# The check of the bounds' bits in a top-k attention kernel: once at the end on a kept copy, not once per batch

## The chip, the cores and the metric

The kernel runs on one core of one Trainium2 chip. The metric is device time in microseconds (us), the median of several runs. The engines are called as in the profile: PE is TensorE (PEld its weight loads), DVE is VectorE, ACT is ScalarE, POOL is GpSimd, SP is SyncE, which issues most DMAs.

## The reference

Eight batches of top-k attention with 8 heads, 576 tokens and a head width of 64, and behind it a mixture-of-depths layer:

```python
scores = scale * np.matmul(q, k.transpose(0, 1, 3, 2))
kth = np.partition(scores, -top_k, axis=-1)[..., -top_k:-top_k + 1]   # top_k = 32
scores = np.where(scores >= kth, scores, -1000000000.0)
...                                                                   # softmax, times v
x = attn_out.transpose(0, 2, 1, 3).reshape(B, S, H * D)               # 8 x 576 x 512
scores = np.einsum('bsd,d->bs', x, w_gate)
out = x.copy()
for b in range(B):
    top_idx = np.argpartition(-scores[b], capacity)[:capacity]        # capacity = 128
    xe = x[b, top_idx]
    ye = np.maximum(xe @ w1, 0.0) @ w2
    out[b, top_idx] = x[b, top_idx] + sigmoid(scores[b, top_idx])[:, None] * ye
```

## The kernel before

**Units.** The attention is cut into 144 units, 18 per batch; a unit is 128 score rows twice (two heads, `i` = 0 and 1), each of 576 scores. The main loop (line 1094) runs over steps `n`, one unit entering at each, and works as a pipeline: in step `n` PE turns the scores of unit n-4 (`weigh`) and multiplies those of unit n+1, ACT takes the exponent (`pT`, `last`), copies the scores out (`sc`), and compares unit n-1 with its bound (`sides`); POOL makes `y` from that and half of the mask `less`; DVE searches.

**The search.** DVE does not look for the 32nd largest score at once. `find_bound` takes a bound near it from parts of the row (maxima of `cand`, then `best`, then `bound`); ACT and POOL work out which scores lie under the bound and how many (`sides`, `seen`, `y`), and `find_kth` takes the 8 largest of `y` (`next8`), the last of which is the 32nd largest. This is exact only if a few things hold. They are gathered as the kernel goes, and checked at the end: `seen` (the counts), `sums` (softmax sums), `ranks`, `others`, and `least`, which is the change's place. If the check fails, the branch at line 1368 computes everything again in a plain way (`general`); with the inputs here it isn't taken.

**The bounds' check.** `keep_least` (line 1073) is called from `mask_of` in the step in which the last unit of a batch gets its mask, for seven batches within the loop, and once more at line 1255. It takes the batch's 36 bounds (18 units, two heads) and 36 32nd-largest values, which lie in `bounds[b]` and `next8s[b]`. DVE looks at the low 23 bits of each bound (`low`: 0 would mean a bound that is a power of two), and reduces bounds, values and `low` to one number each in `least[:, 0:3, b]`.

**The order.** All engines are wrapped in `InOrder`, so each executes its instructions in the order in which the code emits them. Work that is to stand later in an engine's queue is kept in lists of closures: `late` (run by `flush`, mostly ACT's), `vector_late` (`flush_vector`, inside `find_bound`), `pool_late`. In the loop `flush()` stands at line 1127, right behind `mask_of(n - 3)` and ahead of the `sc` copy. The mixture of a batch (`mixture`, line 599) is a generator that is stepped through the loops of the next batches: gate scores (`prod`, line 943, on DVE, which reads `x`, made by POOL), ranks (`junk`), places, rows fetched (`xe`), h and y matmuls.

**The end.** After the loop the last batch's mixture is done by `closing` (line 746), a generator too, with the end of the batch before it (`between`) in it. At its fourth `yield` (line 830, just after `flush()`) the code comes to line 1255: `keep_least` for the last batch, and the chain of reductions that multiplies all checks into `sure`. The following `next(closed)` (line 1295) puts the transposes of `xe` and the `xeT` copy in the queues; `count_unsure()` then puts a matmul of `sure` and `ones` into PE's queue; the next `next(closed)` emits h, y and the scatter of the last rows.

Of the kernel before, what the change touches and what calls it, by code (L numbers as in the profile page):

```python
# [11 lines left out]
ALU = mybir.AluOpType  # L12
FP32 = mybir.dt.float32
BF16 = mybir.dt.bfloat16
I32 = mybir.dt.int32
# [11 lines left out]
LEAST = 1.0e-16 * SMALLER  # L27
# [21 lines left out]
def kernel(  # L49
# [12 lines left out]
    P = nc.NUM_PARTITIONS  # L62
    B, H, S, D = q.shape
# [14 lines left out]
    const = ctx.enter_context(tc.tile_pool(name="const", bufs=1))  # L78
# [4 lines left out]
    stats = ctx.enter_context(tc.tile_pool(name="stats", bufs=6))  # L83
    ptpool = ctx.enter_context(tc.tile_pool(name="pt", bufs=2))
    xpool = ctx.enter_context(tc.tile_pool(name="x", bufs=2))
    modpool = ctx.enter_context(tc.tile_pool(name="mod", bufs=1))
# [43 lines left out]

    NS = B * 2 * (J * NHP + NHP // 2)
    seen = const.tile([P, NS], FP32, name="seen")
    least = const.tile([P, 3, B], FP32, name="least")
    sums = const.tile([P, B * NT, H], FP32, name="sums")
    nc.gpsimd.memset(sums, 1.0)

# [31 lines left out]
    def load_weights():  # L168
# [6 lines left out]
    pe, dve, act, pool, sp = (  # L175
        InOrder(tc, e)
        for e in (nc.tensor, nc.vector, nc.scalar, nc.gpsimd, nc.sync)
    )


    late, vector_late, pool_late = [], [], []
# [5 lines left out]
    def flush():  # L187
        while late:
            late.pop(0)()
# [148 lines left out]
    def groups(t):  # L338

        return NHP // 2 if t == J else NHP  # L340
# [638 lines left out]
    per_batch = sum(groups(t) for t in range(NT))  # L979
# [27 lines left out]
    for b in range(B - 1):  # L1007
        n = (b + 1) * per_batch + mix_at_of.get(b, mix_at)[6]
# [62 lines left out]
        find_kth(ys.pop(n), next8s[b][:, i, :, :])  # L1071

    def keep_least(b, bound, kth):
        low = stats.tile([P, per_batch, 2], I32, name="low", bufs=1)
        dve.tensor_scalar(
            out=low,
            in0=bound.bitcast(I32),
            scalar1=(1 << 23) - 1,
            scalar2=1,
            op0=ALU.bitwise_and,  # L1080
            op1=ALU.bitwise_xor,
        )
        for w, of in enumerate((bound, kth, low)):
            dve.tensor_reduce(
                out=least[:, w, b : b + 1], in_=of, axis=mybir.AxisListType.XY, op=ALU.min
            )

    def mask_of(n, on=None):
        b, i = divmod(n, per_batch)
        masks[n] = mask(scs[n], next8s[b][:, i, :, :], on)  # L1090
        if i == per_batch - 1 and b < B - 1:
            keep_least(b, bounds.pop(b)[:, :, :, 7], next8s.pop(b)[:, :, :, 7])

    for n in range(-1, N):
        b, i = divmod(n, per_batch)
# [32 lines left out]
        if is_unit(n + 1):  # L1128
            b, t, g = units[n + 1]
            ps = room_for_scores()  # L1130
            kT, qT = qkv[b][0:2]
            b, i = divmod(n, per_batch)
# [42 lines left out]
        if gating is not None:  # L1175
            b, t = gating
# [5 lines left out]
        b, i = divmod(n, per_batch)  # L1182
# [70 lines left out]


    keep_least(B - 1, bounds.pop(B - 1)[:, :, :, 7], next8s.pop(B - 1)[:, :, :, 7])
    sure = stats.tile([P, 1], FP32, name="sure")
    dve.memset(sure, 1.0)
    for what, op, than, limit in (
        (least[:, 0, :], ALU.min, ALU.is_gt, LEAST),
        (least[:, 1, :], ALU.min, ALU.is_gt, LEAST),  # L1260
        (least[:, 2, :], ALU.min, ALU.is_gt, 0.5),
        (seen, ALU.max, ALU.is_lt, float(MIDDLE)),
        (seen, ALU.min, ALU.is_gt, float(MIDDLE - 16)),
        (sums.rearrange("p t h -> p (t h)"), ALU.min, ALU.is_gt, FEWEST),
        (sums.rearrange("p t h -> p (t h)"), ALU.max, ALU.is_lt, MOST),
    ):
        far = stats.tile([P, 1], FP32, name="far")
        dve.tensor_reduce(out=far, in_=what, axis=mybir.AxisListType.X, op=op)
        dve.scalar_tensor_tensor(
            out=sure, in0=far, scalar=limit, in1=sure, op0=than, op1=ALU.mult  # L1270
        )
# [133 lines left out]
```

## Time and profile before

| | |
|---|---|
| median of 3 runs | 826.69 us (826.53 to 827.79) |
| the profiled execution | 828.44 us; its span 826.1 us |
| granted TensorE clock over the span | 0.99 of full |
| DVE busy | 787.2 us (95%) |
| POOL busy | 715.4 us (87%) |
| ACT busy | 730.7 us (88%) |
| PE busy | 777.0 us (94%), ends modelled |
| DMA | 50.38 MB, mean 61 GB/s |
| `low` | 8 instructions, 175 / 1060 / 1231 ns (least, median, most) |
| `least` from bounds, values, `low` | 8 each, median 207, 200, 172 ns |

A timeline line reads: start in us from the span's start, duration, engine, source line (L45 is the wrapper, so tiles tell more than lines), operation, output tile <- input tiles, shapes, count; in brackets the idle time of the engine before it and what ended it. A line of waits reads: who waited <- for whom: us in total, times, longest. An engine counts as busy from the start to the end of an instruction, also where the instruction stands still in between.

### The profile page before, as it was taken

What the parts mean: (1) busy time and instruction counts of PE and PEld (TensorE: products, weight loads), DVE (VectorE), ACT (ScalarE), POOL (GpSimd) and SP (SyncE); (2) the same over time, 40 slices, a digit from 0 to 9 for tenths busy, and PEclk for the clock granted to TensorE, in tenths of its full rate; (3) what the DMA queues carried; (4) which work ended last, traced back from release to release, by engine and by line L of the source; (5) the groups of instructions that cost most, each with busy time, mean ns of one, the idle gap of its engine ahead of it and who ended that gap; (6) DMA issues with size and microseconds to landing.
All of it is one profiled execution on the core that took longest, in us unless ns stands there. A gap on an engine that the chain in (4) does not pass through costs nothing. (4 is left out here: it accounts for less than half of the span.)

```text
span 826.1 us, 28252 instructions
## 1 busy us (share of the span) xinstructions
PE 777.0 (94%) x10143; PEld 596.5 (72%) x10143; DVE 787.2 (95%) x4651; ACT 730.7 (88%) x1557; POOL 715.4 (87%) x722
## 2 busy tenths in 40 slices
PE   6888888888999999999999999999999999999976
PEld 5566666666887778877787777877787777767744
DVE  7899999999999999999999999999999999999960
ACT  4799999999999999999999999999999999879831
POOL 3799999999899999999899999999999998899831
PEclk9699999999999999999999999999999999999999
DMA  7931111521141221521223221512215102101021
GB/s 170 283 86 40 28 66 28 105 53 27 60 92 36 53 40 59 112 47 34 79 47 86 53 40 60 104 23 54 40 59 112 28 15 66 23 12 18 2 71 30
DMA packets 122133, 50.38 MB, mean 61 GB/s; under 512 B 116417, under 2 KB 116417, under 8 KB 120961
## 3 DMA queue, kind: packets, MB, share of 16 engines
q1 hardware_dynamic: 118672, 43.91, 22.0%
q0 software_dynamic: 1728, 4.20, 2.8%
q8 instruction: 82, 1.34, 0.8%
q14 instruction: 67, 0.54, 0.3%
q10 hardware_dynamic: 1584, 0.39, 0.2%
HBM read 36.93 MB, written 11.55 MB: 59 GB/s over the span
## 5 line engine op out<-in xcount | busy, mean ns | idle before, releaser
L45 POOL TENSOR_TENSOR y<-sc,sides 128x576 f32<-128x576 f32 x288 | 365.1, 1289 | 57.0 <-ACT sides L45 54.3
L45 DVE MAX8 cand<-sc 128x8 f32<-128x82 f32 (+1 forms) x2016 | 314.0, 228 | 2.7 <-ACT sc L45 2.7
L45 POOL TENSOR_SCALAR less<-sc,next 128x576 bf16<-128x576 f32 x135 | 232.5, 1722 | 12.9 <-DVE next L45 10.0
L45 PE MATMUL ptr<-out_of_reach,less 128*128 128x128 bf16 x1136 | 205.3, 220 | 19.5 <-POOL less L45 19.4
L45 ACT ACTIVATE sides<-sc,bound 128x576 bf16<-128x576 f32 x288 | 223.0, 787 | 0.0
L45 PE MATMUL ptr<-ident,sc 128*128 128x128 f32 x1136 | 217.0, 282 | 0.0
L45 DVE MAX8 next<-y 128x8 f32<-128x584 f32 x288 | 204.4, 751 | 1.7 <-POOL y L45 1.6
L45 PEld LDWEIGHTS av<-v,pT 128*64 128x64 f32 x4544 | 144.1, 137 | 66.9 <-ACT last L45 63.2
L45 PE MATMUL ps<-kT,qT 64*128 64x288 f32 (+1 forms) x1280 | 182.0, 431 | 5.2 <-ACT qT L45 5.2
L45 PEld LDWEIGHTS ptr<-ident,sc 128*128 128x128 f32 x1136 | 161.3, 142 | 29.1 <-issue 17.4
L45 ACT ACTIVATE pT<-ptr 128x1024 f32<-128x1024 f32 x142 | 145.3, 1023 | 33.2 <-PE ptr L45 32.2
L45 PE MATMUL av<-v,pT 128*64 128x65 f32 x4544 | 163.7, 224 | 9.3 <-ACT last L45 8.5
L45 ACT COPY sc<-ps 128x1152 f32<-128x1152 f32 (+1 forms) x144 | 162.2, 1126 | 3.5 <-PE ps L45 3.5
L45 PEld LDWEIGHTS <-less 128*128 128x128 bf16 x1296 | 136.1, 106 | 39.2 <-POOL less L45 25.2
L45 PEld LDWEIGHTS ps<-kT,qT 64*128 64x128 f32 (+1 forms) x1280 | 100.2, 178 | 41.5 <-issue 21.2
L45 ACT ACTIVATE less<-sc,next 128x576 bf16<-128x576 f32 x143 | 111.2, 777 | 12.7 <-DVE next L45 10.8
L45 DVE MATCH_REPLACE8 cand<-best,cand 128x21 f32<-128x21 f32 (+1 forms) x576 | 99.0, 180 | 0.0
L45 DVE MAX8 best<-cand 128x8 f32<-128x21 f32 (+1 forms) x576 | 90.5, 190 | 0.0
L45 PE MATMUL h_ps<-xeT,w 128*128 128x128 f32 x464 | 65.8, 286 | 0.0
L45 PEld LDWEIGHTS h_ps<-xeT,w 128*128 128x128 f32 x464 | 55.8, 191 | 9.2 <-issue 5.8
L45 PE MATMUL y_ps<-w,hT 128*128 128x512 f32 x112 | 60.6, 636 | 0.0
L45 ACT ACTIVATION_READ_ACCUMULATOR sides<-sc,bound 128x1 f32 x288 | 59.9, 208 | 0.0
(133 smaller groups left out, 866.4 us busy)
## 6 DMA issues: line engine op xcount, KB each, us to landing
v<-in_v_dram SPq DMA_DIRECT2D x64, 128.0 KB, 4.2
out_dram<-x SPq DMA_DIRECT2D x8, 1024.0 KB, 3.9
rows<-in_k_dram SPq DMA_DIRECT2D x56, 128.0 KB, 2.9
rows<-in_q_dram SPq DMA_DIRECT2D x56, 128.0 KB, 3.1
w<-in_moe_w_dram SPq DMA_DIRECT2D x2, 2048.0 KB
gate_row<-row_dram SPq DMA_DIRECT2D x7, 288.0 KB, 4.4
w<-in_k_dram SPq DMA_DIRECT2D x8, 128.0 KB, 3.2
last<-in_k_dram SPq DMA_DIRECT2D x8, 128.0 KB, 4.0
```

The costliest lines, as they stand in the source:

```text
L45: return lambda *a, **kw: self._tc.keep_in_program_order(fn(*a, **kw))
```

## The change

Within the loop DVE keeps one reduction per batch, that of the 32nd-largest values. ACT copies the batch's 36 bounds to `bounded`, a tile of 288 numbers that is kept to the end; the copy goes through `late`, and so stands behind ACT's half of the mask and ahead of the `sc` copy. At the end, after the last copy, DVE makes `low` for all 288 bounds in one operation, and the check reduces `bounded` and `low` (288 wide each) and `least` (8 wide) in place of three rows of `least`. `low` shares its space with `junk` and `prod` (tag `scratch`).

```diff
     seen = const.tile([P, NS], FP32, name="seen")
-    least = const.tile([P, 3, B], FP32, name="least")
+    least = const.tile([P, B], FP32, name="least")
+    bounded = const.tile([P, NS], FP32, name="bounded")
...
     def keep_least(b, bound, kth):
-        low = stats.tile([P, per_batch, 2], I32, name="low", bufs=1)
-        dve.tensor_scalar(
-            out=low,
-            in0=bound.bitcast(I32),
-            scalar1=(1 << 23) - 1,
-            scalar2=1,
-            op0=ALU.bitwise_and,
-            op1=ALU.bitwise_xor,
-        )
-        for w, of in enumerate((bound, kth, low)):
-            dve.tensor_reduce(
-                out=least[:, w, b : b + 1], in_=of, axis=mybir.AxisListType.XY, op=ALU.min
-            )
+        at = 2 * per_batch * b
+        late.append(
+            lambda: act.copy(
+                out=bounded[:, at : at + 2 * per_batch].rearrange("p (n i) -> p n i", i=2),
+                in_=bound,
+            )
+        )
+        dve.tensor_reduce(
+            out=least[:, b : b + 1], in_=kth, axis=mybir.AxisListType.XY, op=ALU.min
+        )
...
     keep_least(B - 1, bounds.pop(B - 1)[:, :, :, 7], next8s.pop(B - 1)[:, :, :, 7])
+    flush()
+    low = modpool.tile([P, S], I32, name="low", tag="scratch")[:, 0:NS]
+    dve.tensor_scalar(
+        out=low,
+        in0=bounded.bitcast(I32),
+        scalar1=(1 << 23) - 1,
+        scalar2=1,
+        op0=ALU.bitwise_and,
+        op1=ALU.bitwise_xor,
+    )
     sure = stats.tile([P, 1], FP32, name="sure")
     dve.memset(sure, 1.0)
     for what, op, than, limit in (
-        (least[:, 0, :], ALU.min, ALU.is_gt, LEAST),
-        (least[:, 1, :], ALU.min, ALU.is_gt, LEAST),
-        (least[:, 2, :], ALU.min, ALU.is_gt, 0.5),
+        (bounded, ALU.min, ALU.is_gt, LEAST),
+        (least, ALU.min, ALU.is_gt, LEAST),
+        (low, ALU.min, ALU.is_gt, 0.5),
         (seen, ALU.max, ALU.is_lt, float(MIDDLE)),
```

PE's, POOL's and SP's instructions and their order stay as they were. DVE has three instructions less per batch in the loop; ACT has one more.

## The prediction

> **What bounds the kernel now.** I read the page's first part, then busy time by stretch and waits by engine, one batch, the places where the removed instructions stood, and the end. The page:
>
> ```profile
> PE 777.0 (94%) x10143; PEld 596.5 (72%) x10143; DVE 787.2 (95%) x4651; ACT 730.7 (88%) x1557; POOL 715.4 (87%) x722
> ```
>
> This invites one reading: VectorE (DVE) is the bound, so take work off it. The stretch of one batch in the middle (stretch, length, then busy time of PE, PEld, DVE, ACT, POOL) and all waits of ACT over 0.15 us in it say more:
>
> ```profile
> 392.32:488.42 96.10, 94.93 (x1267) 73.59 (x1266) 95.99 (x577) 91.50 (x197) 88.52 (x88) 1.00 0.27 60
> ```
>
> ```profile
> ACT pT L45 <- PE ptr L45: 4.0, 11, 0.6
> ```
>
> DVE has no gap in 96.1 us. But ACT is busy or waiting for TensorE (91.5 + 4.0) for 95.5 of them, and TensorE's weight loads wait for ACT (8.1 us for `last`). ACT and PE hand work to each other and set 96.1 us as much as DVE does. How can DVE be just as full? The timeline at the end of a batch shows it (start, duration):
>
> ```profile
> 306.11 1.06 DVE L45 TENSOR_SCALAR low<-bound 128x36 int32<-128x36 int32 x1
> 307.10 0.20 DVE L45 TENSOR_REDUCE least<-bound 128x1 f32<-128x36 f32 x1
> 307.23 0.20 DVE L45 TENSOR_REDUCE least<-next 128x1 f32<-128x36 f32 x1
> 307.35 0.17 DVE L45 TENSOR_REDUCE least<-low 128x1 f32<-128x36 int32 x1
> 304.60 2.52 POOL L45 TENSOR_TENSOR y<-sc,sides 128x576 f32<-128x576 f32 x2 [0.84 <-ACT sides L45]
> ```
>
> `low` takes 0.17 us where POOL is idle (113.15) and ends here at 307.17, just after POOL's `y` at 307.12: it stood still for 0.88 us, counted as busy, until POOL let go, and POOL's `y` had waited for ACT. `prod` (line 943) is held in the same way by POOL's `less`:
>
> ```profile
> 419.49 1.71 POOL L45 TENSOR_SCALAR less<-sc,next 128x576 bf16<-128x576 f32 x1
> 419.78 0.99 DVE L45 CUSTOM_DVE_ANT_0 prod<-x,wg 64x512 f32<-64x512 f32 x1
> 461.91 1.73 POOL L45 TENSOR_SCALAR less<-sc,next 128x576 bf16<-128x576 f32 x1
> 462.08 1.12 DVE L45 CUSTOM_DVE_ANT_0 prod<-x,wg 128x512 f32<-128x512 f32 x1
> ```
>
> Both end 1.28 us after the start of `less`, whenever they began. So DVE is tied to POOL, and through POOL to ACT, at some six places per batch.
>
> **What goes out of the loop.** Per batch one `low` and two reductions. From start to start: 0.99 + 0.13 + 0.10 = 1.22 us at 306.11 and alike in four batches, 1.38 at 209.73, 1.16 at 690.56, 0.32 at 113.15: 7.74 us in all. That is the upper bound of the gain. Of it, the first 0.32 is taken back at 119.42, where `prod` stands inside a `y` of POOL until that ends. After the others DVE runs 1.2 us ahead, for 7 to 17 us, until the next `prod`. Reaching 419.78 that much earlier, it meets the `y` that ends at 419.33. Either it gets in there and ends about 0.55 us later (as the one of 77.92 did after the `y` ending 78.64), 0.9 us ahead of now, or it is still held to 1.28 us after `less`, and nothing is left. I take 0.45. The end gains only what ACT no longer waits: `less` on ACT starts late behind DVE's `next` at 407.81 by 0.20 and at 423.88 by 0.25 (0.16 after the start of `last` is usual and counts as no wait). The first goes, the second half: 0.32 a batch. Where DVE does lead, from 720 to 740 (ACT waits 4.9 us for `next`), the 0.45 that is left counts: 0.4.
>
> The Trainium skill, page "SBUF — State Buffer", section "Who interferes with whom", says that a VectorE instruction with two SBUF inputs and a GpSimd instruction that reads SBUF exclude each other for the whole instruction; the rows differ, as `prod` ends 0.43 us before the `less` of 419.49 does. By the page the 0.45 would be nothing, and the time about 1 us longer than my number.
>
> **What comes into the loop.** Seven ACT copies of 128x36, each between `less` and the `sc` copy, behind no wait of its own (its bounds are long there). The trace has no such copy. Nearest: `sums` 128x8 takes 0.21 us with the next instruction 0.12 after its start (745.76, 745.88); `gate_row` 128x64 takes 0.21. Bounds 0.12 and 0.22; I take 0.22, since ACT has no gap there that would hide it: the next wait of ACT comes 20 us later, and PE waits for ACT meanwhile. Queued behind it are the `sc` copy, `xs` and `sides`, and so POOL's `y`. Net 0.10 gained per batch, six batches: 0.6; with the 0.4 above, 1.0 us gained. Bounds: 1.5 lost (seven copies, no gain) to 2.9 gained (six times 0.45 less 0.12, and 0.9).
>
> **The end.** Here the copy stands in ACT's queue behind `gy`, which waits for PE's last `y_ps` (line 742), and the whole check chain on DVE now waits for it. The matmul of `sure` stands in PE's queue ahead of the h matmuls (line 1296):
>
> ```profile
> 802.18 0.45 DVE L45 TENSOR_REDUCE far<-seen 128x1 f32<-128x288 f32 x1
> 804.23 0.69 ACT L45 ACTIVATE gy<-y_ps,g 128x512 f32<-128x512 f32 x1 [2.98 <-PE y_ps L45]
> 804.96 0.16 DVE L45 TENSOR_TENSOR sure<-sure,far 128x1 f32<-128x1 f32 x1
> 805.41 0.19 PE L45 MATMUL av<-ones,sure 128*1 128x1 f32 x2
> 805.52 0.59 ACT L45 COPY xeT<-ptr 128x512 f32<-128x512 f32 x1 [0.60 <-PE ptr L45]
> 806.16 2.05 PE L45 MATMUL ps<-xeT,w 128*128 128x128 f32 x16 [0.56 <-ACT xeT L45]
> ```
>
> Before, the chain ran from 800.93 to 805.12 while DVE had nothing else to do and PE worked on `y_ps`: all hidden. After: the ACT copy starts 0.57 after `gy` does (as 743.86 to 744.43), 804.80; it ends at 805.00; `low` on 288 elements starts at 805.05. Its step is between 0.10 (36 elements, 800.93 to 801.03) and 0.45 (`seen`, 288 elements); I take 0.30. Then `sure`'s memset 0.03; the pair on `bounded`, now 288 wide, 0.56 (802.18 to 802.74 for `seen`); on `least` 0.27; on `low` 0.56; the rest as before, 802.18 to 805.12: 2.94. Sum 4.66: `sure` is ready at 809.71. PE gets it 0.12 later (796.45 to 796.57 for `gate`) and begins h 0.15 after that, at 809.98 in place of 806.16: 3.8 us later (3.6 to 4.0). h, `y` and the last scatter follow one another, so nothing hides this.
>
> **The clock.** PE then has no matmul but transposes and `sure` from 804.19 to 809.98, 5.8 us. Stretches of 3.41 us (length, PE busy, granted clock):
>
> ```profile
> 14.17:17.58 3.41, 2.23 (x19) 1.00 0.92 198
> 17.58:20.99 3.41, 1.54 (x14) 1.00 0.52 114
> 20.99:24.40 3.41, 2.29 (x8) 0.50 0.85 192
> 27.81:31.23 3.42, 2.57 (x15) 0.50 0.97 374
> 31.23:34.64 3.41, 3.41 (x17) 0.50 1.04 414
> 34.64:38.00 3.36, 3.36 (x60) 1.00 1.06 396
> 819.71:823.13 3.42, 0.73 (x2) 1.00 0.03 7
> ```
>
> The clock halved after the stretch that held only transposes (17.58 to 20.99) and after the last (0.73 us of matmuls; 0.50 from 823.13), not after those with 1.24 us of real matmuls (14.17 to 17.58); it came back after the first full one. The edges are equally spaced. However they lie, 5.8 us leave one stretch with at most 0.5 us of matmuls, so I expect the clock to halve. It lasts from 809.98 to the end of the first full stretch: 3.4 to 6.8 us. Eight score matmuls take 2.29 us at half clock and 1.24 at full (21.36, 16.40): 46% of the time is lost, 1.6 to 3.1 us; I take 2.4.
>
> The Trainium skill, page "TensorE: Matmul & The Clock Gate", section "Part 1: The HAM clock gate", gives one idle window of about 3.4 us for the fall and one busy one for the return. By the page alone the fall would need a wholly idle window, and half rate for one window would cost an estimated 1.7 us.
>
> **The sum.** 828.44 (the profiled execution; its span 826.1 and 2.3 around it) - 1.0 + 3.8 + 2.4 = 833.6. The median of the runs is 1.75 below the profiled execution: 831.9.
>
> **Rivals.** (1) The clock stays up: 829.5 (827.4 to 832.2). For it: transposes and `sure` may count for something; before, 2.29 us of PE work from 802.65 to 806.06 kept it. (2) DVE sets the pace, and its lead survives POOL. For it: DVE without a gap, and ACT waiting for `next` from 136 to 200 and from 720 to 740. Against it: the fixed ends of `low` and `prod`. Price: up to 7.7 gained against 6.2 lost, 825.2; without the clock's fall too, 822.8. It decides once more than 6.2 us (3.8 with the clock up) come out of the loop, and then the kernel is faster. (3) The edit moves nothing: excluded for the loop, since DVE's list has three instructions less per batch and ACT's one more, PE's and POOL's are unchanged.
>
> **How the numbers follow.** Forecast 0.75, 829.0 to 835.3 by its bounds; clock up 0.12; DVE's pace 0.13, spread from 822.8 to 829. The range 828.6 to 834.4 leaves out half of DVE's pace, a little of the second case and the worst of the first, some 0.15. A difference under 0.2% (1.65 us) can't be told from none. Faster needs more than 825.0: the far end of DVE's pace, 0.04; within 0.2%: the rest of it below 828.3 and a little of the clock case, 0.09; slower 0.87.
>
> **What would show it.** Right: `sure`'s matmul about 4.4 us behind the transposes of `xe`, h behind it; `low` starting after ACT's copy; half clock in the first h matmuls; batches still of 95.5 to 96.3 us with `prod` pinned to `less`. Wrong: batches of 95 us or less; `sure` ready before 807; PE at full clock through h.

## The result, and the profile after

| | before | after |
|---|---|---|
| median of 6 runs each | 826.61 us (824.87 to 827.79) | 832.12 us (829.61 to 832.6) |
| ratio | | 1.0062 (95%: 1.0049 to 1.0074), 4.1 to 6.1 us more |
| the profiled execution, its span | 828.44, 826.1 us | 832.43, 830.1 us |
| granted TensorE clock over the span | 0.99 | 0.985 |

The kernel is slower, as forecast. The page's first part hides this: it shows a DVE with less to do and 4 us more of span.

```profile
PE 778.5 (94%) x10143; PEld 597.9 (72%) x10143; DVE 785.8 (95%) x4628; ACT 728.4 (88%) x1565; POOL 727.9 (88%) x722
```

DVE is 1.4 us less busy, although up to 7.7 us of work left its loop; POOL, whose instructions are the same 722, is 12.5 us busier. The end, from the timeline (start, duration, engine, operation; in brackets the wait and what ended it):

```profile
802.07 0.69 ACT L45 ACTIVATE gy<-y_ps,g 128x512 f32<-128x512 f32 x1 [2.98 <-PE y_ps L45]
802.66 0.25 ACT L45 COPY bounded<-bound 128x36 f32<-128x36 f32 x1
802.66 0.63 PE L45 MATMUL ptr<-ident,xe 128*128 128x128 f32 x4 [0.63 <-DMA xe<-out_dram,row_i]
802.94 0.31 DVE L45 TENSOR_SCALAR low<-bounded 128x288 int32<-128x288 int32 x1 [3.96 <-ACT bounded L45]
803.32 0.59 ACT L45 COPY xeT<-ptr 128x512 f32<-128x512 f32 x1 [0.42 <-PE ptr L45]
807.33 0.16 DVE L45 TENSOR_TENSOR sure<-sure,far 128x1 f32<-128x1 f32 x1
807.64 0.19 PE L45 MATMUL av<-ones,sure 128*1 128x1 f32 x2 [4.36 <-DVE g L45]
807.76 3.78 PE L45 MATMUL ps<-xeT,w 128*128 128x128 f32 x16
811.34 2.69 PE L45 MATMUL av<-xeT,w 128*128 128x128 f32 x16
813.86 1.95 PE L45 MATMUL h_ps<-xeT,w 128*128 128x128 f32 x16
817.43 7.03 PE L45 MATMUL ps<-w,hT 128*128 128x512 f32 x16
```

Read it as a chain. ACT's copy waits behind `gy`, DVE has stood idle 3.96 us for it, `sure` is done at 807.49, and PE has waited 4.36 us with `xeT` ready since 803.91. The h matmuls then take 3.78 and 2.69 us for what took 2.05 and 1.95. The windows of the clock say why (length, then busy time of PE, PEld, DVE, ACT, POOL, the granted clock, DMA):

```profile
799.22:802.63 3.41, 2.81 (x7) 0.95 (x6) 0.00 (x0) 0.56 (x1) 0.93 (x1) 1.00 0.27 77
802.63:806.04 3.41, 0.63 (x4) 0.42 (x4) 2.93 (x13) 0.86 (x3) 1.62 (x1) 1.00 0.24 11
806.04:809.45 3.41, 1.80 (x10) 1.80 (x11) 1.70 (x12) 0.00 (x0) 0.00 (x0) 0.50 0.40 65
809.45:812.87 3.42, 3.42 (x18) 3.42 (x18) 0.00 (x0) 0.38 (x1) 0.00 (x0) 0.50 0.01 2
812.87:816.28 3.41, 3.41 (x32) 3.41 (x32) 0.00 (x0) 0.77 (x2) 0.00 (x0) 1.00 0.00 0
```

A stretch with 0.63 us of transposes is followed by half clock; half clock ends after the first full stretch.

In the two profiles the 4.0 us of span add up from three places. `gy` starts 2.16 us earlier (804.23 to 802.07). h should then start 2.16 earlier too, at 804.00, but starts at 807.76: 3.76 lost. From the start of h to that of the matmuls of y, at 817.43 above, are 9.67 us; before it was 7.25, as y started at 813.41: 2.42 lost. -2.16 + 3.76 + 2.42 = 4.02.

```profile
813.41 7.03 PE L45 MATMUL ps<-w,hT 128*128 128x512 f32 x16
```

In the middle of the kernel nothing seems to have happened. One batch again, then DVE's groups (operation, tiles, shape, count, busy time, mean ns):

```profile
392.32:488.42 96.10, 94.81 (x1269) 73.41 (x1265) 95.96 (x574) 91.26 (x198) 90.67 (x88) 1.00 0.28 60
```

```profile
L45 DVE CUSTOM_DVE_ANT_0 prod<-x,wg 128x512 f32<-128x512 f32 x32 | 30.4, 950 | 1.4 <-POOL x L45 1.4
L45 DVE TENSOR_SCALAR less<-sc,next 128x576 bf16<-128x576 f32 x10 | 10.2, 1026 | 0.2
L45 DVE TENSOR_SCALAR pick<-slot,ranks 128x128 bf16<-128x128 f32 x7 | 4.3, 621 | 0.3
```

DVE still has no gap (95.96 of 96.10 us). In the same groups of before, `prod` had 29.9 us, and `less` and `pick`:

```profile
L45 DVE TENSOR_SCALAR less<-sc,next 128x576 bf16<-128x576 f32 x10 | 6.7, 675 | 0.2
L45 DVE TENSOR_SCALAR pick<-slot,ranks 128x128 bf16<-128x128 f32 x7 | 2.4, 340 | 0.3
```

Where the freed time stands is seen in a timeline of after, with the POOL instruction that holds DVE, and of before:

```profile
390.29 2.52 POOL L45 TENSOR_TENSOR y<-sc,sides 128x576 f32<-128x576 f32 x2
391.92 1.22 DVE L45 TENSOR_SCALAR less<-sc,next 128x576 bf16<-128x576 f32 x1
392.76 0.44 POOL L45 TENSOR_TENSOR y<-steps,seen 128x16 f32<-128x16 f32 x1
```

```profile
390.36 2.52 POOL L45 TENSOR_TENSOR y<-sc,sides 128x576 f32<-128x576 f32 x2
392.85 0.21 POOL L45 TENSOR_TENSOR y<-steps,seen 128x16 f32<-128x16 f32 x1
393.33 0.50 DVE L45 TENSOR_SCALAR less<-sc,next 128x576 bf16<-128x576 f32 x1
```

Before, DVE came to its share of `less` at 393.33, after POOL's `y`. Now it comes 1.41 us earlier, into the middle of `y`, and stands until that ends at 392.81; then POOL's small `y` stands behind DVE (0.44 in place of 0.21). That is also where most of POOL's added busy time is: its small `y` takes 43.0 us in sum (32.2 before), its `less` 236.9 (232.5). Both engines count as busy while they stand.

What ACT waits for, from 30 to 790 us, tells what the early DVE is worth. Before, and after:

```profile
ACT pT L45 <- PE ptr L45: 32.2, 75, 1.6
ACT less L45 <- DVE next L45: 10.8, 15, 2.7
```

```profile
ACT pT L45 <- PE ptr L45: 37.1, 80, 1.6
ACT less L45 <- DVE next L45: 5.8, 10, 1.1
```

ACT waits 5.0 us less for DVE and 4.9 us more for PE: what it gained from the earlier DVE it lost again in waiting for another engine.

### The profile page after: what moved, and what is told of

It is laid out like the page before. It is cut to its first block, busy times and chain, and to the rows that moved or that the text cites. A ratio compares the mean times of both kernels' runs of the same rounds, so it can differ in the third digit from the quotient of the medians.

```text
span 830.1 us, 28237 instructions
## 1 busy us (share of the span) xinstructions
PE 778.5 (94%) x10143; PEld 597.9 (72%) x10143; DVE 785.8 (95%) x4628; ACT 728.4 (88%) x1565; POOL 727.9 (88%) x722
## 5 line engine op out<-in xcount | busy, mean ns | idle before, releaser
L45 POOL TENSOR_SCALAR less<-sc,next 128x576 bf16<-128x576 f32 x135 | 236.9, 1755 | 3.3 <-DVE next L45 2.2
L45 ACT ACTIVATE pT<-ptr 128x1024 f32<-128x1024 f32 x142 | 145.2, 1023 | 38.9 <-PE ptr L45 37.1
```

Source lines behind the costliest of these rows:

```text
L45: return lambda *a, **kw: self._tc.keep_in_program_order(fn(*a, **kw))
```

## The experiments

All against the kernel before, each group on one chip: 825.35 us there for the first four, 825.89 for the next four, 826.59 for the last two. "Over" and "under" are the ratio's interval times that median. In the edits shown, `...` stands for lines left out.

| kernel | ratio (95%) | us against before |
|---|---|---|
| `before_wait` | 1.0077 (1.0064 to 1.009) | +5.3 to +7.4 |
| `pe_busy` | 1.0043 (1.003 to 1.0056) | +2.5 to +4.6 |
| `sure_last` | 1.0025 (1.0014 to 1.0036) | +1.2 to +3.0 |
| `dve_copy` | 0.9997 (0.9987 to 1.0007) | -1.1 to +0.6 |
| `no_low` | 0.9989 (0.9981 to 0.9998) | -1.6 to -0.2 |
| `dve_more` | 1.0014 (1.0004 to 1.0024) | +0.3 to +2.0 |
| `copy4` | 1.004 (1.0026 to 1.0054) | +2.1 to +4.5 |
| `sure_mid` | 0.9979 (0.9967 to 0.999) | -2.7 to -0.8 |
| `sure_mid_2` (the same again) | 0.9993 (0.9981 to 1.0004) | -1.6 to +0.3 |
| `dve_mid` | 0.9986 (0.9974 to 0.9999) | -2.1 to -0.1 |

The theory: the end costs all of it, by a wait in PE's queue and the clock that falls in it, and the loop gains little, as ACT and PE set its pace. Rival A: ACT's copies in the loop cost the time. Rival B: DVE sets the loop's pace, and the end ate a gain of several us.

**The wait without the change: `before_wait`.** The kernel before, its loop untouched, with idle work on DVE ahead of the check:

```diff
+    for _ in range(12):
+        idle = stats.tile([P, 1], FP32, name="idle")
+        dve.tensor_reduce(out=idle, in_=seen, axis=mybir.AxisListType.X, op=ALU.max)
     sure = stats.tile([P, 1], FP32, name="sure")
```

> The kernel before with 12 more reductions of `seen` (288 wide) on VectorE ahead of the check chain, about 4.4 us that nobody reads; the loop is untouched. Theory: `sure` is ready near 809.5, h starts 3.6 us later and runs at half clock for a while: 826.6 + 3.6 + 2.4 = 832.6. Rival B (wait alone): 830.2. Rival A (the loop's copies are the cost): 826.6, as there are none.

831.13 us, 5.3 to 7.4 over. Its timeline:

```profile
806.46 0.19 PE L45 MATMUL av<-ones,sure 128*1 128x1 f32 x2 [4.12 <-DVE g L45]
806.57 3.78 PE L45 MATMUL ps<-xeT,w 128*128 128x128 f32 x16
810.15 2.16 PE L45 MATMUL av<-xeT,w 128*128 128x128 f32 x16
```

The wait and the slow matmuls are there, and the whole loss, without one copy in the loop. The end alone is enough; rival A is not needed.

**The wait without the clock's fall: `pe_busy`.** The changed kernel, with 64 idle matmuls ahead of that of `sure`:

```diff
+        for _ in range(64):
+            pe.matmul(ps[:, 0:P], out_of_reach, out_of_reach)
         pe.matmul(ps[0:1, 0:1], sure, ones)
```

> The changed kernel with 64 small bf16 matmuls on constants in PE's queue between the transposes of `xe` and the matmul of `sure`; they take some 3.6 us and write a bank that `sure` then overwrites. The wait for `sure` stays, the stretch without matmuls goes. Theory: the clock stays up, h takes 7.3 us and not 9.7, time 832.1 - 2.4 = 829.7. Rival B (the clock costs nothing): 832.1, or more if the matmuls delay `sure`.

828.72 us, 2.5 to 4.6 over. `sure` comes no earlier, but h runs at full clock:

```profile
802.23 3.74 PE L45 MATMUL av<-out_of_reach 128*128 128x128 bf16 x64
806.67 0.19 PE L45 MATMUL av<-ones,sure 128*1 128x1 f32 x2 [0.70 <-DVE ones L45]
806.79 2.05 PE L45 MATMUL ps<-xeT,w 128*128 128x128 f32 x16
```

The granted clock is 1.00 in every stretch of 3.4 us from 797.9 to 808.1, and h takes 7.24 us, not 9.67. By the medians the idle matmuls win back 0.0062 - 0.0043, 1.6 us (the two intervals leave -0.6 to +3.6); by the trace 2.4. So the price of the clock rests on the traces. What remains is the wait of 3.8 less the loop's gain.

**The wait away, three ways.** `dve_copy` lets DVE copy the last batch's bounds itself, ahead of `gy`; the other seven copies stay on ACT:

```diff
...
-    keep_least(B - 1, bounds.pop(B - 1)[:, :, :, 7], next8s.pop(B - 1)[:, :, :, 7])
+    keep_least(
+        B - 1, bounds.pop(B - 1)[:, :, :, 7], next8s.pop(B - 1)[:, :, :, 7], dve.tensor_copy
+    )
```

> The changed kernel with one edit: the last batch's 36 bounds are copied by VectorE itself, not by ScalarE behind `gy`. The chain is as long as in the changed kernel (4.7 us), but starts about 4 us earlier. Theory (the place in ScalarE's queue makes it late): `sure` is ready about 0.5 us after the transposes of `xe` at most, PE has no long stretch without matmuls, and the time is within 0.5 us of the kernel with `sure` last, about 826. Rival C (the chain is too long for the gap, wherever it starts): above 830.

825.14 us, level with before: the end's loss is gone (0.0062 + 0.0003 of 826 is 5.4 us against the changed kernel). `sure` still arrives after the transposes, but no later than `xeT`, and h follows 0.06 us behind the end of that copy (803.49 to 804.07).

```profile
803.71 0.19 PE L45 MATMUL av<-ones,sure 128*1 128x1 f32 x2 [0.26 <-DVE g L45]
804.13 2.05 PE L45 MATMUL ps<-xeT,w 128*128 128x128 f32 x16 [0.23 <-ACT xeT L45]
```

`sure_last` moves the matmul of `sure` behind y:

```diff
     next(closed)
-    count_unsure()
     next(closed, None)
+    count_unsure()
```

> The changed kernel with the matmul of `sure` put behind h, y and the scatter instead of ahead of h, so that no engine waits for the longer check chain; the copies and the loop stay as changed. Theory (the end costs 3.8 us of waiting and 2.4 us of half clock, the loop gains about 2): 832.1 - 6.2 = 826, about 1 to 2 us under the kernel before. Rival A (the copies on ScalarE cost the time, inside the loop): it stays near 832. Rival B (the wait alone, the clock costs nothing): 828.3.

827.54 us, 1.2 to 3.0 over, where 1 to 2 us under before was expected: a miss. h starts at 802.59 at full clock, so wait and clock are gone. But the flag for the branch at the end (`unsure`) is made only when the last rows (`gy`) are:

```profile
816.91 0.75 DVE L45 SCALAR_TENSOR_TENSOR gy<-ps,g,xe 128x512 f32<-128x512 f32 x1 [10.57 <-PE ps L45]
817.58 0.13 DVE L45 TENSOR_SCALAR unsure<-av 1x1 int32<-1x1 f32 x1
817.94 1.01 POOL L45 DMA_INDIRECT out_dram<-gy,row_i  x1 [14.37 <-DVE unsure L45]
```

From the scatter's start to the end of the span are 6.4 us, in before 4.5 (821.59 to 826.1); the scatter lands 4.8 us after its issue in place of 3.0. The DMA view of 817.6 to 820 shows three packets on the queues that it calls `instruction`:

```profile
q8 instruction: 1, 0.02, 4.4%
q14 instruction: 2, 0.02, 3.6%
```

From 806 to 817.6 there were none; before, with its flag known at 805.78, had four in this stretch. The Trainium skill, page "Runtime: NRT & Kernel Launch", section "Instruction fetch mechanics", says that a taken branch outside the fetched window must first fetch its target. The packets fit that, but nothing in the trace says which of them are the branch's, and before has packets on these queues beside its last scatter too (five from 820 on). So that the late branch makes the 1.9 us is argued, not shown. With the loop's 1.0 gained, 1.9 would make 0.9 over, where 1.2 to 3.0 were measured: part of this kernel's time may be open besides.

`sure_mid` puts it between the two, behind h and ahead of y, by one more `yield` in `closing`:

```diff
             act.activation(
                 hT[:, f0 : f0 + 2, :],
...
+        yield
         ps = room_for_scores()[:, 0, 0, :]
...
     next(closed)
+    next(closed)
     count_unsure()
```

> The changed kernel with the matmul of `sure` behind the h matmuls and ahead of those of y. `sure` is ready some 3.8 us after h could begin, and h takes 7.2 us, so no wait is left, PE never falls idle, and the load of the branch's flag ends well before the last scatter. Theory: all of the end's 6.2 us is gone, the loop's gain is left: 0.5 to 1.5 us under the kernel before. Rival A (the copies in the loop cost time): over the kernel before by 1 or more.

> The changed kernel with only the matmul of `sure` moved between h and y, once more, on the chip of the kernel with the copies on DVE, so that the two can be compared and the loop's gain be told more closely. 1.7 us under the kernel before was measured; 0.8 to 2.0 expected again. If the loop's gain is the 1.0 of the prediction: nearer 1.0.

824.43 us on one chip (0.8 to 2.7 under), 826.05 on another (1.6 under to 0.3 over, where 0.8 to 2.0 under was expected). Nothing waits for `sure` now, and the flag is there 7.9 us ahead of the last scatter (817.57):

```profile
801.91 2.05 PE L45 MATMUL ps<-xeT,w 128*128 128x128 f32 x16 [0.68 <-ACT xeT L45]
809.25 0.19 PE L45 MATMUL av<-ones,sure 128*1 128x1 f32 x2
809.48 0.15 DVE L45 TENSOR_SCALAR unsure<-av 1x1 int32<-1x1 f32 x1 [3.73 <-PE av L45]
```

This is the changed kernel with one matmul moved; by the medians it beats the changed kernel by 5.7 to 6.9 us (0.9993 and 0.9979 against 1.0062), and the one before on one chip of two.

**What the loop holds.** `no_low` is the kernel before without `low` and without the reductions of bounds and `low` in seven batches; those batches' bounds are not checked. (The check's `low` is 0 for a bound whose low 23 bits are 1, not for a power of two: the XOR with 1 turns 0 into 1.)

```diff
...
+        if b < B - 1:
+            dve.tensor_reduce(
+                out=least[:, 1, b : b + 1], in_=kth, axis=mybir.AxisListType.XY, op=ALU.min
+            )
+            return
         low = stats.tile([P, per_batch, 2], I32, name="low", bufs=1)
```

> The kernel before, with `low` and the reductions of bounds and `low` left out of the loop and nothing put in their place (the bounds of seven batches are not checked; no copy, the end as before): the upper bound of what the loop can give. Theory (the freed 1.2 us per batch becomes standing still at later DVE instructions that POOL holds): 0.5 to 2 us under the kernel before, busy time of DVE less than 3 us below before's, DVE's `less` and `pick` longer than before's 0.42 and 0.20 us. Rival B (DVE sets the pace): 7.4 to 7.7 us under the kernel before, all of it in the loop.

0.2 to 1.6 under: of up to 7.7 us of DVE work about 0.9 turns into time, with no copy and no new end. Its DVE is busy 785.4 us, 1.8 less than before, and `less` again holds a part of what was freed:

```profile
L45 DVE TENSOR_SCALAR less<-sc,next 128x576 bf16<-128x576 f32 x10 | 10.2, 1028 | 0.2
```

Another part stands in the wide `prod` (33.5 us, 29.9 before). `pick`, which was expected to be longer too, is not (mean 348 ns, 340 before).

`dve_more` goes the other way, three reductions of 128x288 more per batch:

```diff
...
+        if b < B - 1:
+            for _ in range(3):
+                idle = stats.tile([P, 1], FP32, name="idle")
+                dve.tensor_reduce(out=idle, in_=spare, axis=mybir.AxisListType.X, op=ALU.max)
         low = stats.tile([P, per_batch, 2], I32, name="low", bufs=1)
```

> The kernel before with three idle reductions of a 128x288 constant tile on DVE ahead of `low` in each of seven batches: 7.8 us of DVE work more, nothing else changed. Theory (DVE's place is set by POOL; `low` stands still 0.88 us there already, and the rest delays what follows): `low` shrinks to about 0.2 and takes in some 0.8 of the 1.1 us per batch; 0 to 3 us over the kernel before. Rival B (DVE sets the pace): 7 to 8 us over.

0.3 to 2.0 over. From start to start they take 1.07 us a batch, 7.5 in all; 1.2 of it is seen. Most of the rest went into `low`, which now comes after POOL's `y` and no longer stands still (mean 214 ns, before 855):

```profile
L45 DVE TENSOR_SCALAR low<-bound 128x36 int32<-128x36 int32 x8 | 1.7, 214 | 0.0
```

So 7.7 us off DVE or 7.5 onto it move the kernel by about 1. Rival B falls, in both directions.

`copy4` puts four copies of the bounds on ACT per batch and takes nothing away:

```diff
...
+        if b < B - 1:
+            at = 2 * per_batch * b
+            to = bounded[:, at : at + 2 * per_batch].rearrange("p (n i) -> p n i", i=2)
+            for _ in range(4):
+                late.append(lambda: act.copy(out=to, in_=bound))
```

> The kernel before with four ACT copies of the 36 bounds in each of seven batches (28 copies, at the place where the changed kernel has one), nothing taken away and the end as before. At about 0.16 us from start to start they take 4.5 us of ACT. If a copy at this place delays everything by its whole length: 4.5 us over the kernel before, and the changed kernel's seven copies cost 1.1 us. If ACT has slack behind it: 0 to 1 us over, and the copies of the changed kernel cost nothing. I lean to 2 to 4.5.

2.1 to 4.5 over. The four copies take longer than assumed, 1.03 us from the first's start to the next instruction (405.75 to 406.78):

```profile
405.75 1.12 ACT L45 COPY bounded<-bound 128x36 f32<-128x36 f32 x4
406.78 1.11 ACT L45 COPY sc<-ps 128x1152 f32<-128x1152 f32 x1
```

Seven times 1.03 are 7.2 us of ACT, of which 3.3 show: nearly half. By the medians a microsecond put on ACT costs three times what one put on DVE does (3.3 of 7.2 against 1.2 of 7.5; the intervals leave 30 to 62% against 4 to 26%). For the changed kernel's single copy, 0.16 us from start to start (306.98 to 307.14), that makes an estimated 0.07 a batch, 0.5 in all. One thing more shows here: DVE's `less` (10.2 us) and POOL's busy time (727.9) rise as in the changed kernel, although nothing was taken from DVE. This fits that the two meet by how far DVE runs ahead of ACT and POOL, not by how much work it has.

`dve_mid` takes `sure_mid` and moves all copies to DVE:

```diff
...
-        late.append(
-            lambda: act.copy(
-                out=bounded[:, at : at + 2 * per_batch].rearrange("p (n i) -> p n i", i=2),
-                in_=bound,
-            )
-        )
+        dve.tensor_copy(
+            out=bounded[:, at : at + 2 * per_batch].rearrange("p (n i) -> p n i", i=2),
+            in_=bound,
+        )
```

> The changed kernel with the matmul of `sure` between h and y, and with all eight copies of the bounds on DVE in place of ACT (at the place of the reductions). If ACT's copies, 0.16 us each from start to start, stand on the path, as three quarters or so of those four times as many did, taking them off ACT gains 0.5 to 1.1 us against the kernel that has only the matmul moved. If they have no price, the two are equal within 0.3 us. For DVE the copy (some 0.1 us) is less than what it stands still now. Rival B (DVE sets the pace): 0.7 us slower than the kernel with only the matmul moved.

825.62 beside 826.05 us: 0.4 under `sure_mid_2`, which the intervals don't tell from nothing. Unlike what was expected, the copy does not take 0.1 us:

```profile
304.04 1.05 DVE L45 COPY bounded<-bound 128x36 f32<-128x36 f32 x1
302.52 2.51 POOL L45 TENSOR_TENSOR y<-sc,sides 128x576 f32<-128x576 f32 x2 [0.83 <-ACT sides L45]
```

It stands in POOL's `y` to its end at 305.03, as `low` did there; at the end of `dve_copy`, with POOL idle, it takes 0.18. The Trainium skill, page "SBUF — State Buffer", section "Who interferes with whom", names copies beside `tensor_scalar` among the operations that can take the port pair shared with GpSimd; this row agrees.

With DVE held there again, `less` takes 6.6 us in sum and POOL is busy for 715.8, as before, and ACT waits 10.8 us for DVE's `next` and 31.6 for PE's `ptr`, where `sure_mid_2` has 6.8 and 35.9. The time is the same within the intervals: the exchange of one wait for the other is worth nothing that these runs can tell.

## Why the prediction was right

**The loop: size within what the runs leave open, way wrong in part.** The prediction had 1.0 us gained (bounds 1.5 lost to 2.9 gained). The runs with the end mended give 0.2 (`dve_copy`), 1.7 and 0.6 (`sure_mid` twice) under before. The ratio of the changed kernel, 5.1 us over, less the 6.2 of the end, gives 1.1. The 2.16 of the two profiles can't be taken for the loop's gain: `before_wait`, whose loop is unchanged, also reaches `gy` 3.13 us earlier than the profile of before, 2.06 of it by the end of the first batch and most of the rest in the stretch from 690 to 745, where ACT waits 5.4 us for `next` in before, 3.9 in `before_wait` and 1.3 after.

The profiles say more if the first batch is left out, from ACT's `sc` copy of unit 18 to the start of the last `gy`. The two with the old loop (before, `before_wait`) take 704.2 and 703.1 us, the six with the changed one 701.4 to 702.5: 0.6 to 2.8 gained, 1.7 by the means. Five batches (units 36 to 126, by the same copies) hold 0.08 a batch of it, where 0.10 net was taken; the batch ahead of them holds 0.5, and what comes behind unit 126 0.9, where 0.4 was taken. Single profiles are coarse, though: `no_low` gains 2.1 by this measure and 0.2 to 1.6 by its runs. By the medians of the runs, the loop's gain stays open between 0.2 and 1.7.

**DVE tied to POOL: right, by other instructions.** The prediction gave `prod` the part of taking DVE's lead away and left 0.45 of it. The trace shows the sum of `prod` hardly changed: its 40 instructions take 38.7 us, 39.4 before. At 419.78 the first branch of its alternative came true, DVE gets in ahead of POOL's `less`:

```profile
419.01 0.65 POOL L45 TENSOR_TENSOR y<-steps,seen 128x16 f32<-128x16 f32 x1
419.65 1.71 POOL L45 TENSOR_SCALAR less<-sc,next 128x576 bf16<-128x576 f32 x1
418.65 0.94 DVE L45 CUSTOM_DVE_ANT_0 prod<-x,wg 64x512 f32<-64x512 f32 x1
```

`prod` ends at 419.59, 1.18 us earlier than before (0.9 was written for this branch), and POOL's small `y` stands in its place: the sign "`prod` pinned to `less`" did not come. The lead lives on to DVE's own `less` and `pick`. Per batch, from start to start in the five batches above, `low` and its two reductions took 1.25 us; `less` goes from 0.42 to 1.13 and `pick` from 0.20 to 0.68, 1.19 more, and `prod` takes 0.15 less: 1.04 of the 1.25 is taken back. The result is alike, since DVE could gain only what ACT no longer waits for, and ACT then waited for PE (10.8 to 5.8, and 32.2 to 37.1; `before_wait`, with the old loop, has 9.3 and 33.8, so a part of this differs between executions). That step, "the end gains only what ACT no longer waits", held. One price beside it does not add up: were nothing left of the 0.45, the prediction's own terms would lose 0.32 in each of six batches and the 0.4, 2.3 us in all, not the "about 1 us" that it wrote.

**The copies: oversized.** 0.22 was taken for one, 1.3 in the sum; the traces have 0.16, of which less than half shows by the estimate from `copy4`.

**The end: right to a tenth.** The wait was 3.76 us (3.8 taken), the chain from `low` to `sure` 4.55 (4.66): the step of `low` on 288 elements was 0.23, not 0.30.

**The clock: right.** 2.42 us lost (2.4 taken, 1.6 to 3.1). It lasted 6.83 us, two stretches, of which h filled 5.1. Rival (1), the clock staying up, was `pe_busy`: that kernel lies 3.6 over before, where 829.5 - 826.7 = 2.8 was written for it.

**The median.** The sum for the profiled execution was 833.6, and it took 832.43: the loop's gain in that pair of profiles was larger. The median came out at 832.1 (831.9 forecast) because this execution lay 0.3 above its median, not 1.75 as that of before. That the two differences cancel is luck; by the ratio, 5.1 us (4.1 to 6.1) stand against 5.2 forecast.

## What to carry to other kernels

An engine that is busy for 95% may be standing still in another's instructions: compare the durations of one operation at several places before work taken off it is counted as time, and ask which wait of the next engine gets shorter. When a check is gathered at the end, look at what stands behind it in an in-order queue: here one 0.19 us matmul ahead of the last matrix products cost 3.8 us by its wait and 2.4 by the clock that fell in it. Such a matmul belongs where its input is long ready and its result is needed late, but not last: between h and y it cost nothing that the runs can tell, behind y the end took 1.9 us longer.

## What the runs showed of the hardware that was not expected

- Instructions of DVE and POOL that met lengthened each other both ways: DVE's `less` went from 0.50 to 1.22 us inside POOL's `y`, and POOL's 128x16 `y` from 0.21 to 0.44 and 0.65 us, with DVE's `less` or `prod` begun ahead of it. Busy time of POOL rose by 12.5 us with no instruction added.
- A 128x36 copy on ACT took 0.25 us and 0.16 from start to start, but four into the same place took 1.03, not 0.64.
- With the flag of the branch made only at the last scatter, that scatter landed 4.8 us after its issue, not 3.0, and 6.4 us passed from its start to the end of the span, against 4.5. Why is open.
